# Two groups of a fused FNet and SwiGLU block: TensorE's units in another order

## The chip, the core and the metric

The kernel runs on one core of one Trainium2 chip. The core has a matrix engine (TensorE; PE in the profile, with its weight loads in a row of their own, PEld), three engines for elementwise work (VectorE or DVE, ScalarE or ACT, GpSimd or POOL) and an engine that mainly issues loads and stores (SyncE or SP). Each engine runs its own list of instructions in order and waits for the others on semaphores. TensorE writes its results into eight banks of PSUM, 128 x 512 floats each; ACT and DVE read them out into the main on-chip memory, SBUF.

The metric is the device time of one execution in microseconds (us). The time before is the median of three runs, 693.0 us, from 691.73 to 693.62.

## The reference, cut to what matters

One sequence of 2048 rows of width 512 goes through a Fourier mixing layer and then through a gated feed-forward layer of inner width 1792, both behind a layer norm that is modulated by a conditioning vector:

```python
mod = (_silu(c) @ w_mod).reshape(c.shape[0], 6, 1, -1)
sa, ca, ga, sb, cb, gb = (mod[:, 0], mod[:, 1], mod[:, 2], mod[:, 3], mod[:, 4], mod[:, 5])
h = _layernorm(x, axis=-1) * (1 + ca) + sa
x = x + ga * _A_ref(h, A_dft_seq_re, A_dft_seq_im, A_dft_hid_re, A_dft_hid_im)
h = _layernorm(x, axis=-1) * (1 + cb) + sb
x = x + gb * _B_ref(h, B_w1, B_w3, B_w2)

def _B_ref(x, w1, w3, w2):
    gate = jnp.einsum("bsd,df->bsf", x, w1)
    up = jnp.einsum("bsd,df->bsf", x, w3)
    h = _silu(gate) * up
    out = jnp.einsum("bsf,fd->bsd", h, w2)
    return out
```

The change touches only the second layer, `_B_ref`.

## The kernel before, in words

**Splitting.** TensorE multiplies rounded numbers, so each operand is kept as a high part (the value rounded) and a low part (what the rounding left over), and every product takes three matmuls: high by high, high by low, low by high (`product`, line 98; its matmuls are all on line 100). ACT makes the high parts (`copy`, line 87) and DVE the low ones (`minus`, line 90). So a new operand costs one instruction on each of the two, and the low part waits for the high one.

**Tiles and groups.** The 2048 rows are four tiles t of 512, taken as two pairs, (0, 2) and (1, 3). The inner width is seven slices g of 256. A group is one slice for one pair. The list `items` has twelve groups, numbered here 0 to 11: slices 2 to 6 for the first pair (groups 0 to 4), then slices 0 to 6 for the second (groups 5 to 11). Group 5 is "the turn" (`turning` is 5), group 6 the one behind it, group 11 the last.

**Units.** Within a group, w1's and w3's blocks are multiplied by a scheme with seven products in place of eight (`factor`): a1 to a7 are w1's, b1 to b7 are w3's. A unit has six matmuls of 512 columns. Products of one operand add up in the same bank: w1's in banks 0 to 2 and w3's in banks 3 to 5. So a6 adds onto a1's bank 0, a7 onto that and a4 onto that, and between two of them ACT copies the bank out (`x<-bank`, line 87), or DVE adds it to such a copy (`plus`, line 93). w3's results are then multiplied by w1's (`times`, line 96), and what comes out is split for the next step (`hf`). w1's results go through the Silu on ACT (line 1244).

**Second products.** A unit y multiplies such results by w2. For groups 5 to 9 there are seven of them, again by the scheme of seven products (`seven_unit`), in the order 2, 5, 3, 1, 6, 7, 4. All use banks 6 and 7. After each, ACT reads both banks out, scaled by `gb` (`copy_by`, line 335, two instructions `y<-bank,gb`), and POOL adds the pair to a sum in device memory (line 1352). Products 3, 6, 7 and 4 add onto what 5 or 1 left in the banks, so they too must wait until the copy of the one before is out. For groups 10 and 11 there are eight plain units (`down_unit`), whose results DVE adds directly (line 1146); once w1's products of group 11 are done, they go round over five banks (6, 7, 0, 1, 2).

**Order.** What runs when is set by a string for each group, read from left to right, in program order for all engines; a unit that begins with `-` belongs to the group before. `y` takes the next second product from the queue `seconds`, which still holds those of the group before. Behind each unit two things are put in. Steps that `behind(n, ...)` deferred by n units go first (the splits above are such steps). Then comes preparation from the queue `jobs`: the coming weights are split (`w1h`, `w1l`) and so are their sums (`w1s`, `w1sh`, `w1sl`), as much of it as `beside` finds room for by a fixed account of 1.36 us for each unit. So the string sets the places of the ACT and DVE instructions too.

The strings before (the second `body` holds for groups 6 to 9, with a `y` put in behind a6 in groups 7 to 9, whose head, as group 10's, is the second; group 10 has a body of its own; line 1795 and on):

```python
        body = "a6 a5 y y a7 y a3 y a4 y b1 y b2 y b6 b5 y"
        if i and items[i - 1] in SEVEN:
            body = "a6 a5 a7 y a3 a4 y b1 b2 y b6 b5 y"
        ...
        if i == len(items) - 1:
            body = "a6 a5 a7 a3 a4 b1 b2 y b6 y b5 y b7 y b4 y y b3 y y y y y y y y y y"
        head = "-b7 a1 -b4 -b3 a2 " if i == turning else "-b7 a1 a2 -b4 -b3 " if i else "a1 a2 "
        if spread and i < len(items) - 1:
            head = "-b7 a1 y a2 -b4 y -b3 "
        if i == len(items) - 1:
            head = "-b7 y a1 a2 y -b4 y -b3 "
```

## Time and profile before

| | |
|---|---|
| time, median of 3 runs | 693.0 us (691.73 to 693.62) |
| the profiled execution's own time | 692.95 us |
| its span, first to last instruction | 691.2 us |
| TensorE busy | 675.1 us, 98% of the span |
| TensorE weight loads | 558.0 us, 81% |
| VectorE busy | 586.5 us, 85% |
| ScalarE busy | 451.5 us, 65% |
| GpSimd busy | 132.8 us, 19% |

The profile is of one execution. Its page sums up each engine, and its other views show the single instructions in order of time (the timeline), whom each engine waited for (the waits) and the busy time by stretch of the span (the windows). All times in them are counted from the start of the span. In a row of the timeline stand the start, the length, the engine, the line of the kernel, what is written and read, and in brackets the idle time before it with the instruction that ended it. Instructions of one kind that follow each other are merged into one row (x2). Consecutive matmuls overlap, so their pace is read from start to start. The groups' places in the span: group 6's a6 starts at 500.80, the last group's a6 at 645.68.

### The profile page before, as it was taken

To read this page: it belongs to the slowest core of one execution; us is meant where nothing else is said; L and a number is where in the kernel's file an instruction comes from. 1 tells how busy PE (TensorE), PEld (TensorE's weight loads), DVE (VectorE), ACT (ScalarE), POOL (GpSimd) and SP (SyncE) were. 2 spreads that over 40 slices of the span, in tenths; PEclk is the share of its full clock that TensorE was granted. 3 is DMA by queue.
4 is the path that set the end of the run, shared out by engine and by line. 5 is a ranking of instruction groups with operands and counts; after the bars stand their busy time and mean duration, and the time that the engine had idled before them with its cause. 6 is when DMAs were issued, how large, how long until landed. Compare 5 with 4: busy or idle time off the path is not lost.

```text
span 691.2 us, 9031 instructions
## 1 busy us (share of the span) xinstructions
PE 675.1 (98%) x3122; PEld 558.0 (81%) x3122; DVE 586.5 (85%) x945; ACT 451.5 (65%) x751; POOL 132.8 (19%) x156
## 2 busy tenths in 40 slices
PE   7999899999999999999999999999999999999996
PEld 5899788888888888888788888887878888888785
DVE  5999769997999988889997989787998979888375
ACT  4998956555353665663577767867677887877520
POOL 1320252543435000010101001011002112221100
PEclk9999999999999999999999999999999999999999
DMA  8730289787588541273667666376939898899803
GB/s 269 216 125 1 67 307 360 260 299 255 186 308 277 166 151 30 46 139 122 97 164 140 150 152 121 92 133 118 277 74 210 166 202 168 177 217 173 191 28 126
DMA packets 40261, 116.80 MB, mean 169 GB/s; under 512 B 5136, under 2 KB 5392, under 8 KB 40208
## 3 DMA queue, kind: packets, MB, share of 16 engines
q0 software_dynamic: 14512, 50.86, 36.5%
q1 hardware_dynamic: 25264, 63.98, 27.9%
q10 hardware_dynamic: 432, 1.31, 0.5%
q8 instruction: 26, 0.43, 0.3%
q14 instruction: 27, 0.22, 0.1%
HBM read 76.81 MB, written 41.42 MB: 171 GB/s over the span
## 4 chain that ended last, share of the span: by engine, by line
PE 83%; DVE 8%; ACT 4%; DMA 2%; issue 1%; SPq 1%; another core or an unknown queue 1%; DVEq 0%; ACTq 0%
PE bank L100 55%; PE bank L750 25%; PE bank L559 1%; DMA wmr<-in_wmr 1%; PE bank L598 1%; SPq L231 1%; DVE xr L805 1%; DVE ul L90 1%; DVE hl L90 0%; ACT hm L501 0%; DMA w<-in_wdi 0%; ACT hh L87 0%; PE bank L576 0%; PE bank L485 0%
## 5 line engine op out<-in xcount | busy, mean ns | idle before, releaser
L100 PE MATMUL bank<-hf,w2h 128*128 128x512 f32 (+1 forms) x352 | 108.3, 389 | 0.0
L87 ACT ACTIVATE hf<-v 128x512 fp32r<-128x512 f32 x71 | 44.4, 631 | 67.3 <-DVE v L96 56.5
L335 ACT ACTIVATE y<-bank,gb 128x512 f32<-128x512 f32 x118 | 76.6, 683 | 4.2 <-PE bank L100 3.6
L100 PEld LDWEIGHTS bank<-hf,w2h 128*128 128x128 f32 x352 | 65.6, 188 | 15.3 <-ACT y L335 1.4
L1160 POOL DMA_DIRECT2D sum<-y x28 | 24.1, 859 | 240.7 <-ACT y L335 124.5
L100 PE MATMUL bank<-hf,w2l 128*128 128x512 f32 (+1 forms) x176 | 68.1, 387 | 0.0
L90 DVE TENSOR_TENSOR hf<-v,hf 128x512 fp32r<-128x512 f32 x71 | 48.7, 686 | 10.3 <-ACT hf L87 10.3
L1352 POOL DMA_DIRECT2D sum<-y x35 | 29.9, 854 | 128.8 <-ACT y L335 119.7
L87 ACT ACTIVATE x<-bank 128x512 f32<-128x512 f32 x72 | 41.9, 593 | 13.3 <-PE bank L100 12.5
L750 PE MATMUL bank<-d,us 128*128 128x512 f32 x128 | 49.9, 390 | 0.1
L750 PE MATMUL bank<-bh,us 128*128 128x512 f32 x128 | 49.9, 390 | 0.0
L750 PE MATMUL bank<-bh,ul 128*128 128x512 f32 x128 | 49.9, 389 | 0.0
L750 PE MATMUL bank<-d,uh 128*128 128x512 f32 x128 | 49.8, 389 | 0.0
L750 PE MATMUL bank<-l,us 128*128 128x512 f32 x128 | 49.8, 389 | 0.0
L750 PE MATMUL bank<-l,uh 128*128 128x512 f32 x128 | 49.8, 389 | 0.0
L170 POOL DMA_INDIRECT re<-in_ctr,mirror x32 | 35.6, 1111 | 64.3 <-DVE ul L90 38.5
L170 POOL DMA_INDIRECT im<-in_cti,mirror x32 | 33.4, 1044 | 36.3 <-PE bank L750 8.7
L93 DVE TENSOR_TENSOR x<-bank,x 128x512 f32<-128x512 f32 x36 | 24.7, 686 | 17.8 <-PE bank L100 17.8
L100 PEld LDWEIGHTS bank<-hf,w2l 128*128 128x128 f32 x176 | 33.1, 188 | 6.7
L1244 ACT ACTIVATE v<-v 128x512 f32<-128x512 f32 x36 | 22.7, 629 | 23.1 <-DVE v L93 22.7
L93 DVE TENSOR_TENSOR v<-bank,x 128x512 f32<-128x512 f32 x36 | 24.7, 686 | 14.9 <-PE bank L100 14.0
L100 PE MATMUL bank<-h2h,w1h 128*128 128x512 f32 x80 | 31.1, 389 | 0.0
(260 smaller groups left out, 1904.2 us busy)
## 6 DMA issues: line engine op xcount, KB each, us to landing
sum<-y POOLq DMA_DIRECT2D x63, 512.0 KB
w<-in_w SPq DMA_DIRECT2D x42, 512.0 KB
re<-in_ctr SPq DMA_DIRECT2D x32, 256.0 KB
im<-in_cti SPq DMA_DIRECT2D x32, 256.0 KB
wmc<-in_wmc SPq DMA_DIRECT2D x8, 512.0 KB
xr<-in_xt SPq DMA_DIRECT2D x8, 512.0 KB
sum<-xr SPq DMA_DIRECT2D x8, 512.0 KB
x<-in_x SPq DMA_DIRECT2D x11, 256.0 KB
```

The costliest lines, as they stand in the source:

```text
L87: nc.scalar.activation(dst, src, AF.Copy, scale=scale)
L90: nc.vector.tensor_tensor(out=dst, in0=a, in1=b, op=OP.subtract)
L93: nc.vector.tensor_tensor(out=dst, in0=a, in1=b, op=OP.add)
L100: nc.tensor.matmul(acc, lhs[a], rhs[b], start=first and n == 0, stop=last and n == len(PASSES) - 1, skip_group_check=more,)
L170: nc.gpsimd.indirect_dma_start(dst, None, rows, bass.IndirectOffsetOnAxis(ap=at, axis=0))
L231: queue.dma_start(raw_w[dt][q * 64 : (q + 1) * 64, m, :], w[i][par::2, q])
L335: nc.scalar.activation(dst, src, AF.Identity, scale=by)
L559: nc.tensor.matmul(halves(hb[k])[:, m, :], sides((hh, hl)[a][k])[:, dt, m, :], wu[dt][:, b, m, :], start=False, stop=dt % 2 == 1 and n == ...
L750: nc.tensor.matmul(acc[what, e], lhs, rhs, start=begin and i == 0, stop=(end or (turn and what == "x")) and i == len(terms) - 1, skip_grou ...
L1160: nc.gpsimd.dma_start(sums[t, d // 2], y, accum_op=OP.add)
L1244: behind(k != 0 or q == 0, lambda: nc.scalar.activation(v, src, AF.Silu))
L1352: nc.gpsimd.dma_start(sums[t, which], y, accum_op=OP.add)
```

## The change

The string of group 6 gets a line of its own, and the last group's string is written anew; nothing else is touched:

```diff
@@ -1798,6 +1798,8 @@
         body = "a6 a5 y y a7 y a3 y a4 y b1 y b2 y b6 b5 y"
         if i and items[i - 1] in SEVEN:
             body = "a6 a5 a7 y a3 a4 y b1 b2 y b6 b5 y"
+        if i == turning + 1:
+            body = "a6 a5 y a7 a3 y a4 b1 y b2 b6 y b5"
         spread = i > 1 and items[i - 2] in SEVEN
@@ -1806,7 +1808,7 @@
         if i == len(items) - 1:
-            body = "a6 a5 a7 a3 a4 b1 b2 y b6 y b5 y b7 y b4 y y b3 y y y y y y y y y y"
+            body = "a6 a5 b1 a7 a3 b2 a4 y b6 y b5 y b7 y b4 y y b3 y y y y y y y y y y"
```

In group 6 each of its four y units comes one unit sooner. Two other units stand between neighbours as before, except behind the fourth: from there to the next y (in group 7's head, `-b7 a1 y`) there are three in place of two. In the last group b1 moves from behind a4 to between a5 and a7, and b2 from behind b1 to between a3 and a4. Instructions and transfers are the same ones in number and size.

**First place: ACT in group 6.** Shown are ten rows from the Silu of w1's product a7 on, before (`hf` are high parts of right-hand factors, `w1h` and `w1sh` high parts of the next group's weights and of their sums, `y` the copies out of banks 6 and 7):

```order
L1244 ACTIVATE v_717_4580<-v_717_4580 128x512
L335 ACTIVATE y_731_4655<-bank6_729_4653,gb_152 128x512
L335 ACTIVATE y_731_4655<-bank7_730_4654,gb_152 128x512
L87 ACTIVATE hf_732_4665<-v_661_4308 128x512
L87 ACTIVATE w1h_734_4677<-w1_718_4582 128x1024
L87 ACTIVATE hf_736_4684<-v_661_4308 128x512
L1244 ACTIVATE v_716_4579<-v_716_4579 128x512
L1244 ACTIVATE v_717_4580<-bank0_714_4571 128x512
L87 ACTIVATE w1sh_738_4696<-w1s_735_4679 128x1024
L335 ACTIVATE y_741_4701<-bank6_739_4699,gb_152 128x512
```

The same stretch of ACT now, from the copies of the first y on:

```order
L335 ACTIVATE y_730_4644<-bank6_728_4642,gb_152 128x512
L335 ACTIVATE y_730_4644<-bank7_729_4643,gb_152 128x512
L87 ACTIVATE hf_731_4654<-v_660_4307 128x512
L87 ACTIVATE hf_732_4664<-v_661_4308 128x512
L1244 ACTIVATE v_717_4580<-v_717_4580 128x512
L87 ACTIVATE w1h_734_4677<-w1_718_4582 128x1024
L87 ACTIVATE hf_736_4684<-v_661_4308 128x512
L1244 ACTIVATE v_716_4579<-v_716_4579 128x512
L335 ACTIVATE y_739_4689<-bank6_737_4687,gb_152 128x512
L335 ACTIVATE y_739_4689<-bank7_738_4688,gb_152 128x512
L87 ACTIVATE w1sh_741_4701<-w1s_735_4679 128x1024
```

The first pair of copies now stands ahead of the Silu of a7, and the second pair ahead of `w1sh`, with the Silu from bank 0 (a4's) behind it.

**Second place: ACT and DVE at the end of group 6 and the head of group 7.** ACT before, from the third y's copies to the fifth's (`x<-bank3` is the copy of b6, `hf` the high part of the result of group 6's b7, `x<-bank0` the copy of group 7's a1):

```order
L335 ACTIVATE y_749_4741<-bank7_740_4700,gb_152 128x512
L87 ACTIVATE w2sh_751_4753<-w2s_747_4734 128x1024
L87 ACTIVATE x_744_4721<-bank3_743_4714 128x512
L87 ACTIVATE w3h_753_4765<-w3_733_4675 128x1024
L87 ACTIVATE x_755_4774<-bank5_754_4767 128x512
L335 ACTIVATE y_759_4783<-bank6_757_4781,gb_152 128x512
L335 ACTIVATE y_759_4783<-bank7_758_4782,gb_152 128x512
L87 ACTIVATE w3sh_761_4795<-w3s_756_4776 128x1024
L87 ACTIVATE hf_762_4805<-v_717_4580 128x512
L87 ACTIVATE x_764_4814<-bank0_763_4807 128x512
L335 ACTIVATE y_769_4823<-bank6_757_4781,gb_152 128x512
```

ACT now, from the high part of b2's result on, which stands behind the third y's copies there:

```order
L87 ACTIVATE hf_749_4749<-v_716_4579 128x512
L87 ACTIVATE x_744_4721<-bank3_743_4714 128x512
L87 ACTIVATE w2sh_751_4760<-w2s_748_4744 128x1024
L335 ACTIVATE y_754_4765<-bank6_752_4763,gb_152 128x512
L335 ACTIVATE y_754_4765<-bank7_753_4764,gb_152 128x512
L87 ACTIVATE w3h_756_4777<-w3_733_4675 128x1024
L87 ACTIVATE x_758_4786<-bank5_757_4779 128x512
L87 ACTIVATE hf_760_4801<-v_717_4580 128x512
L87 ACTIVATE x_762_4810<-bank0_761_4803 128x512
L87 ACTIVATE w3sh_767_4818<-w3s_759_4788 128x1024
L335 ACTIVATE y_768_4821<-bank6_752_4763,gb_152 128x512
```

b6's copy has moved from behind the third y's copies and `w2sh` to ahead of `w2sh`, and `w3sh` from ahead of b7's `hf` and the copy of a1 to behind them, right ahead of the fifth y's copies.

DVE before, in the same stretch (`x<-bank3` and the product `v` behind it are the two steps on b7's result):

```order
L90 TENSOR_TENSOR w3s_756_4776<-w3_733_4675,w3s_756_4776 128x256
L90 TENSOR_TENSOR w3l_760_4793<-w3_733_4675,w3h_753_4765 128x1024
L93 TENSOR_TENSOR x_755_4774<-bank3_743_4714,x_755_4774 128x512
L96 TENSOR_TENSOR v_717_4580<-v_717_4580,x_755_4774 128x512
L90 TENSOR_TENSOR w3sl_768_4820<-w3s_756_4776,w3sh_761_4795 128x1024
L90 TENSOR_TENSOR hf_762_4805<-v_717_4580,hf_762_4805 128x512
```

DVE now:

```order
L90 TENSOR_TENSOR w3s_759_4788<-w3_733_4675,w3s_759_4788 128x256
L93 TENSOR_TENSOR x_758_4786<-bank3_743_4714,x_758_4786 128x512
L96 TENSOR_TENSOR v_717_4580<-v_717_4580,x_758_4786 128x512
L90 TENSOR_TENSOR w3l_766_4816<-w3_733_4675,w3h_756_4777 128x1024
L90 TENSOR_TENSOR hf_760_4801<-v_717_4580,hf_760_4801 128x512
L90 TENSOR_TENSOR w3sl_769_4831<-w3s_759_4788,w3sh_767_4818 128x1024
```

On DVE the two steps on b7's result have moved ahead of `w3l`.

**Third place: TensorE in the last group.** The last three matmuls of a5 and the first three behind it, before:

```order
L100 MATMUL bank2_976_5937<-th_667_4343,w1sh_941_5750 128x512
L100 MATMUL bank2_976_5937<-tl_672_4360,w1sh_941_5750 128x512
L100 MATMUL bank2_976_5937<-th_667_4343,w1sl_942_5760 128x512
L100 MATMUL bank0_962_5859<-th_671_4358,w1sh_941_5750 128x512
L100 MATMUL bank0_962_5859<-tl_675_4373,w1sh_941_5750 128x512
L100 MATMUL bank0_962_5859<-th_671_4358,w1sl_942_5760 128x512
```

and now:

```order
L100 MATMUL bank2_976_5937<-th_667_4343,w1sh_941_5750 128x512
L100 MATMUL bank2_976_5937<-tl_672_4360,w1sh_941_5750 128x512
L100 MATMUL bank2_976_5937<-th_667_4343,w1sl_942_5760 128x512
L100 MATMUL bank3_978_5946<-h2h_625_4122,w3h_950_5803 128x512
L100 MATMUL bank3_978_5946<-h2l_628_4133,w3h_950_5803 128x512
L100 MATMUL bank3_978_5946<-h2h_625_4122,w3l_955_5823 128x512
```

Before, a7 came next and added onto bank 0, which a6 had filled one unit earlier; now b1 comes next, in bank 3, and a7 one unit later.

## The prediction

> **What bounds the kernel now.** I read the page first, then whom TensorE waited for in the part with the changed groups, then the timeline of each engine around those waits. From the page:

> ```profile
> PE 675.1 (98%) x3122; PEld 558.0 (81%) x3122; DVE 586.5 (85%) x945; ACT 451.5 (65%) x751; POOL 132.8 (19%) x156
> ...
> PEclk9999999999999999999999999999999999999999
> ...
> PE 83%; DVE 8%; ACT 4%; DMA 2%; issue 1%; SPq 1%; another core or an unknown queue 1%; DVEq 0%; ACTq 0%
> ```

> TensorE is busy 98% of the span at full clock, and 83% of the chain that ends last is its own work. A new order leaves its matmuls what they are. It can only take away or add waits between them. The view of waits, from 480 us to the end, has these rows (who waited for whom, total, times, longest):

> ```profile
> POOL sum L1352 <- DMA sum<-y: 9.0, 2, 4.6
> ...
> PEld bank L100 <- ACT y L335: 1.9, 3, 1.0
> PEld bank L100 <- ACT x L87: 1.0, 2, 0.5
> ```

> So TensorE's weight loads, which run ahead of the matmuls, were held up five times in this whole stretch, three times by copies of second products and twice by copies of w1's or w3's. Of the compute engines only POOL waits for a transfer. Here are four of the five places in TensorE's timeline (start, length), with the rows around them, and one place without a wait (526.36) for later:

> ```profile
> 512.61 0.39 PE L100 MATMUL bank<-h2l,w3h 128*128 128x512 f32 x1
> 512.84 0.39 PE L100 MATMUL bank<-h2h,w3l 128*128 128x512 f32 x1
> 513.76 0.73 PE L100 MATMUL bank<-hf,w2sh 128*128 128x512 f32 x2 [0.53 <-ACT y L335]
> ...
> 519.12 0.39 PE L100 MATMUL bank<-hf,w2l 128*128 128x512 f32 x1
> 519.63 0.50 PE L100 MATMUL bank<-th,w3sh 128*128 128x512 f32 x1
> 519.97 0.40 PE L100 MATMUL bank<-tl,w3sh 128*128 128x512 f32 x1
> ...
> 526.36 0.39 PE L100 MATMUL bank<-th,w3l 128*128 128x512 f32 x1
> 526.59 0.63 PE L100 MATMUL bank<-hf,w2sh 128*128 128x512 f32 x2
> ...
> 639.26 0.39 PE L100 MATMUL bank<-h2h,w1l 128*128 128x512 f32 x1
> 639.76 0.74 PE L100 MATMUL bank<-hf,w2sh 128*128 128x512 f32 x2
> ...
> 648.18 0.39 PE L100 MATMUL bank<-th,w1sl 128*128 128x512 f32 x1
> 648.56 0.50 PE L100 MATMUL bank<-th,w1sh 128*128 128x512 f32 x1
> ```

> The pace is 0.23 us from start to start (512.61 to 512.84), so a unit of six takes 1.36. Whatever is above the pace is a wait. A wait also costs the next matmul 0.11: it comes 0.34 behind the first (519.63 to 519.97), and a pair behind a wait lasts 0.73, not 0.63 as at 526.59. That gives:

> - A, group 6's third y at 513.76: 0.92 - 0.23 + 0.11 = 0.80
> - B, group 6's b7 at 519.63: 0.51 - 0.23 + 0.11 = 0.39
> - C, the last group's a7 at 648.56: 0.38 - 0.23 + 0.11 = 0.26
> - D, a y in the head of the last group at 639.76: 0.50 - 0.23 + 0.11 = 0.38, and the fifth held-up load, of the next y there

> D lies ahead of the new string, in units that it leaves alone. A, B and C together are 1.45 us, the most that the change can gain.

> **What makes A, B and C.** The timelines of ACT and DVE there:

> ```profile
> 507.40 0.63 ACT L1244 ACTIVATE v<-v 128x512 f32<-128x512 f32 x1 [1.17 <-DVE v L93]
> ...
> 509.08 0.63 ACT L87 ACTIVATE hf<-v 128x512 fp32r<-128x512 f32 x1
> 509.60 1.06 ACT L87 ACTIVATE w1h<-w 128x1024 fp32r<-128x1024 f32 x1
> ...
> 511.59 0.59 ACT L1244 ACTIVATE v<-bank 128x512 f32<-128x512 f32 x1
> 512.07 1.06 ACT L87 ACTIVATE w1sh<-w1s 128x1024 fp32r<-128x1024 f32 x1
> 513.02 1.26 ACT L335 ACTIVATE y<-bank,gb 128x512 f32<-128x512 f32 x2
> ...
> 516.35 0.63 ACT L87 ACTIVATE hf<-v 128x512 fp32r<-128x512 f32 x1 [0.63 <-DVE v L96]
> ...
> 518.98 0.60 ACT L87 ACTIVATE x<-bank 128x512 f32<-128x512 f32 x1
> ...
> 522.21 1.06 ACT L87 ACTIVATE w3sh<-w3s 128x1024 fp32r<-128x1024 f32 x1
> 524.62 0.63 ACT L87 ACTIVATE hf<-v 128x512 fp32r<-128x512 f32 x1 [1.34 <-DVE v L96]
> ...
> 525.63 1.26 ACT L335 ACTIVATE y<-bank,gb 128x512 f32<-128x512 f32 x2
> ...
> 647.39 0.63 ACT L87 ACTIVATE hf<-v 128x512 fp32r<-128x512 f32 x1 [2.03 <-DVE v L96]
> 647.93 1.27 ACT L87 ACTIVATE x<-bank 128x512 f32<-128x512 f32 x2
> ```

> ```profile
> 502.54 0.69 DVE L90 TENSOR_TENSOR hf<-v,hf 128x512 fp32r<-128x512 f32 x1
> ...
> 506.08 0.69 DVE L90 TENSOR_TENSOR v<-v,v 128x512 f32<-128x512 f32 x1
> ...
> 513.16 1.23 DVE L90 TENSOR_TENSOR w1sl<-w1s,w1sh 128x1024 fp32r<-128x1024 f32 x1 [0.64 <-ACT w1sh L87]
> ...
> 522.04 1.22 DVE L90 TENSOR_TENSOR w3l<-w,w3h 128x1024 fp32r<-128x1024 f32 x1
> 523.17 0.68 DVE L93 TENSOR_TENSOR x<-bank,x 128x512 f32<-128x512 f32 x1
> 523.89 0.69 DVE L96 TENSOR_TENSOR v<-v,x 128x512 f32<-128x512 f32 x1
> ```

> ACT's copies of the second y are last in a queue that ACT works off without a gap from 507.40; they begin at 513.02, and the third y starts 0.74 later (A). The copy of b6 ends at 518.98 + 0.60 = 519.58, behind an `hf`, the third y's pair and `w2sh`, and b7 starts 0.05 later (B). In the last group the copy of a6 stands behind an `hf` that waits for b3's result, and a7 comes right after a6's copy (C). All three are waits for ACT's place in line; none is for data that come from memory.

> **Group 6.** Each y comes one unit sooner, so A's copies get the same two units of room, but the queue ahead of them is shorter. Before, ACT idled 1.17 ahead of the Silu at 507.40, waiting for a7's result; now the first y's pair (1.14) runs in that gap. a7's own result comes later, since a7 is one unit later: on DVE it now stands two steps behind the one at 506.08, at 0.6 to 0.72 each, and is done near 508.1. From the Silu to `w1sh` ACT took 512.07 - 507.40 = 4.67. The same rows stand in between now but for one `hf` (0.52, from 509.08 to 509.60) and the Silu of a4 (0.48, from 511.59 to 512.07), so `w1sh` begins near 508.1 + 3.67 = 511.8, and the pair of the second y two places of 0.57 ahead of it, at 510.65. Its first bank is free at 510.65 + 0.74 = 511.39. The third y, the tenth unit of the string before, would have started at 512.84 + 0.23 = 513.07 without its wait; as the ninth it wants to start at 511.71. A is gone, with 0.3 to spare. b6's copy now stands right behind the `hf` that began at 516.35, ahead of `w2sh` and the pair; that `hf` waits for DVE, which is 0.3 sooner there (below), so the copy runs from about 516.6 to 517.2. b7 wants it at 513.07 + 4 x 1.36 = 518.5: B is gone, with 1.3 to spare. The first y, now the third unit, starts at 513.07 - 7 x 1.36 = 503.55 and needs a factor whose low part DVE finishes at 502.54 + 0.69 = 503.23; it holds, by 0.3. Gain 0.80 + 0.39 = 1.19.

> **What is late next.** TensorE now reaches group 7 1.19 sooner, and the sixth y of the queue (526.59 before) wants banks 6 and 7 at 525.40. Before, it did not wait, but only just: the fifth y's pair began at 525.63, and 525.63 + 0.74 = 526.37. Its pair hangs on DVE, which has no slack there:

> ```profile
> 513.00:528.00 15.00, 14.35 (x62) 11.32 (x62) 14.22 (x22) 12.92 (x21) 3.37 (x4) 1.00 0.86 168
> 528.00:540.00 12.00, 12.00 (x55) 9.93 (x54) 8.99 (x16) 9.60 (x18) 2.60 (x4) 1.00 1.03 208
> ```

> (stretch, its length, busy time of PE, PEld, DVE, ACT and POOL, then clock and DMA, for this stretch and the next). DVE works 14.22 of 15 us. So b7's two steps, which ended at 523.89 + 0.69 = 524.58, come sooner only by what the new order gives: `w1sl` waits for `w1sh`, 0.3 sooner, and `w3l` (523.17 - 522.04 = 1.13) now stands behind them. That is 523.15, and `hf` on ACT at 523.2. But ACT now has `w3sh` (0.95, 512.07 to 513.02) between `hf` and the pair, where it had run it in an idle stretch before. The pair begins at 523.2 + (525.63 - 524.62) + 0.95 = 525.16, its first bank is free at 525.90, and the sixth y waits 525.90 - 525.40 = 0.50, plus 0.11: it gives back 0.61. The bounds of this cost are zero, if `hf` comes by 522.7, and 527.32 - 525.40 + 0.11 = 2.03, if b7's steps come no sooner than before (524.62 + 1.01 + 0.95 + 0.74 = 527.32). I take 0.61, which goes by the order of rows on both engines. Behind group 7's head the strings are the old ones, and I carry the rest of the gain to the end at no loss: from 528 on DVE works 8.99 and ACT 9.60 of 12 us, so what they are behind they make up.

> **The last group.** b1 goes into bank 3, which group 10's b4 left four units earlier, and w3's parts for it are split while group 10 runs. It covers the copy of a6: that ends near 649.2 in the worst case (647.93 + 1.27), and a7 now starts at 648.18 + 0.23 + 1.36 = 649.8. C is gone: 0.26. b2 one unit sooner also makes w2's split sooner by one unit, which nobody waits for. a4 now stands right ahead of the first y, whose banks go round 7, 0, 1, 2, 6; the second y overwrites a4's bank 0 two units later (2.72), and ACT needs 0.6 to read it. I cost these at nothing. If ACT were held up, 2.1 us of cover would go first.

> The loads by SP and the adds by POOL are the same ones; the four adds of group 6 are issued about one unit sooner and no transfer moves past another.

> **The sum.** -0.80 - 0.39 + 0.61 - 0.26 = -0.84 against the profiled execution's own 692.95, which is 0.05 below the median of 693.0. On the median: 692.2.

> [...] The trace shows 0.11 behind each wait, and in the view of waits it is the weight loads that wait. [...]

> **The rivals.**

> 1. The wait at the sixth y does not come, since `hf` is out by 522.7, for instance because DVE saves more than 0.3 at `w1sl`. Against it stands `w3sh` ahead of the pair and DVE's 14.22 of 15. Gain 1.45: 691.5.
> 2. Slower: the same wait is larger than what was gained. This happens if DVE ends b7's two steps later than 524.0: then hf at 524.05, the pair at 526.0, its bank at 526.74, and 526.74 - 525.40 + 0.11 is 1.45. At its worst (524.58, as before) the wait is 2.03, the sum +0.58, the time 693.6. For it: one late ACT result (`w3h` or `w2sh`, which DVE's low parts wait for) delays everything behind it on a full DVE. Against it: the new order on DVE has b7's steps ahead of `w3l`, and this needs 0.85 more than I laid out.
> 3. The group gives all back and no more: the y's wait is 1.19 wherever exactly, since a DVE without slack sets the pace from 513 to 528, and only C remains. Then -0.26: 692.7.

> **How the numbers follow.** The likeliest case, with a wait of 0.3 to 1.0 at the sixth y, has 0.6 and gives 691.8 to 692.5; rival 1 has 0.15, rival 2 has 0.1, rival 3 has 0.15. All of them lie within 0.3% (2.1 us) of 693.0, which is about what a measurement of this kernel can tell from no change: its three runs lie 1.9 us apart. The chances of faster and slower by more than that come from that scatter alone and from what I overlook: 0.08 faster, since the likeliest cases lean that way, 0.06 slower, 0.86 within. The range must take in rivals 1 to 3 and about half the runs' scatter: 691.2 to 693.6.

> **What would show it right or wrong.** In TensorE's timeline of the changed kernel the gaps A, B and C are closed, and there is a new gap of 0.3 to 1.0 ahead of the sixth y, near 526, that the waits put down to ACT's `y`; on ACT `w3sh` stands right before the fifth y's pair without a gap. D stays as it is. If the second y's pair on ACT begins after 511, A is not gone. If the gap is near 2, rival 2 holds. The prediction would be wrong altogether if a new wait showed up in groups 8 to 10, whose order is untouched, or in the tail behind 655.

## The result and the profile after

The changed kernel takes 694.13 us (median of 22 runs, 693.24 to 696.26), beside 693.0 for the kernel before (22 runs, 691.73 to 694.03). The ratio is 1.0017, with a 95% interval of 1.0011 to 1.0023: 1.2 us slower, where 0.8 us faster was forecast, and outside the forecast range. The profiled execution took 694.64 us. From the changed kernel's page:

```profile
span 692.9 us, 9028 instructions
...
PE 674.7 (97%) x3122; PEld 558.9 (81%) x3122; DVE 586.9 (85%) x945; ACT 451.8 (65%) x751; POOL 132.0 (19%) x156
...
q8 instruction: 26, 0.43, 0.3%
q14 instruction: 28, 0.23, 0.1%
...
PE 84%; DVE 9%; ACT 2%; DMA 2%; issue 1%; SPq 1%; ACTq 0%; DVEq 0%
```

Nothing here says where the time went: the same engine, the same work, a busy time 0.4 us less than before. Two small things have moved, the number of instructions and q14, one of the two queues that the page calls `instruction`. On the page of the kernel before they read:

```profile
span 691.2 us, 9031 instructions
...
q8 instruction: 26, 0.43, 0.3%
q14 instruction: 27, 0.22, 0.1%
```

Three instructions fewer, and one packet of 8 KB more. Both lead to the loss, but first the part on which the prediction rests.

**TensorE.** The view of waits from 480 us on has one row for TensorE's weight loads, and the row for copies of w1's and w3's products (`x L87`) is gone:

```profile
PEld bank L100 <- ACT y L335: 1.9, 3, 1.0
```

In TensorE's timeline (start, length) of the changed kernel, at the third y, at b7, at the sixth y, at D and at the last group's a7:

```profile
512.13 0.62 PE L100 MATMUL bank<-hf,w2sh 128*128 128x512 f32 x2
512.59 0.39 PE L100 MATMUL bank<-hf,w2sl 128*128 128x512 f32 x1
...
518.71 0.39 PE L100 MATMUL bank<-th,w3sl 128*128 128x512 f32 x1
518.93 0.39 PE L100 MATMUL bank<-th,w3sh 128*128 128x512 f32 x1
...
525.50 0.39 PE L100 MATMUL bank<-th,w3l 128*128 128x512 f32 x1
526.46 0.74 PE L100 MATMUL bank<-hf,w2sh 128*128 128x512 f32 x2 [0.56 <-ACT y L335]
...
639.28 0.39 PE L100 MATMUL bank<-h2h,w1l 128*128 128x512 f32 x1
639.78 0.74 PE L100 MATMUL bank<-hf,w2sh 128*128 128x512 f32 x2
...
649.56 0.39 PE L100 MATMUL bank<-h2h,w3l 128*128 128x512 f32 x1
649.78 0.39 PE L100 MATMUL bank<-th,w1sh 128*128 128x512 f32 x1
```

The third y starts at the pace (its pair lasts 0.62, the length of a pair without a wait), b7 follows 0.22 behind the matmul ahead of it, a7 likewise: A, B and C are gone. D is as it was (0.50). There is one new wait, at the sixth y: 526.46 - 525.50 = 0.96, less 0.23, plus 0.11 behind it, is 0.84.

**The whole stretch.** The two profiled executions differ ahead of the change: by 0.53 us at one and the same wait in group 2. That is chance, since kernels with the same orders ahead of this wait lie as far apart there (342.38 in lg, 342.92 before). So TensorE is measured from there. Of the kernel before, the matmul behind that wait and the last matmul:

```profile
342.92 0.50 PE L100 MATMUL bank<-th,w3sh 128*128 128x512 f32 x1 [0.36 <-ACT x L87]
...
684.00 0.28 PE L100 MATMUL bank<-hf,w2l 128*128 128x256 f32 x1
```

and of the changed one:

```profile
343.45 0.50 PE L100 MATMUL bank<-th,w3sh 128*128 128x512 f32 x1 [0.36 <-ACT x L87]
...
683.74 0.28 PE L100 MATMUL bank<-hf,w2l 128*128 128x256 f32 x1
```

341.08 before, 340.29 now: TensorE gained 0.79 us, where 0.84 was forecast. Even with its late start it ends 0.26 earlier than before. Laid matmul by matmul beside the kernel before, 0.07 of the 0.79 is there already at group 6's a6, ahead of the change. Up to the sixth y another 1.31 is gained, the wait there and the units just behind it give back 0.87, and the last group gains 0.29. So the change itself is worth 0.72.

**The tail.** Behind the start of the last matmul the span of the kernel before goes on for 691.2 - 684.00 = 7.2 us, that of the changed one for 692.9 - 683.74 = 9.2. These 2.0 us are the loss: -0.79 + 1.96 = 1.17, and the medians differ by 0.17% of 693, which is 1.18. The tail has no matmul, no add and no output that is late. What it has is in the view of transfers from 685.5 us to the end, here the bandwidth in 40 slices of 0.24 us and the packets of q14, first of the kernel before:

```profile
GB/s 26 267 285 285 280 39 108 52 4 0 0 0 0 0 34 0 34 0 0 0 0 0 0 0 0 0 0 0 0 0 0 0 0 0 0 0 0 0 0 0
...
q14 instruction: 4, 0.03, 1.3%
```

then of the changed kernel:

```profile
GB/s 358 190 367 91 30 129 13 0 0 0 0 0 0 34 0 34 0 0 0 0 0 0 0 0 0 34 0 0 0 0 0 0 0 0 0 0 0 0 0 0
...
q14 instruction: 5, 0.04, 1.6%
```

The high numbers at the left are the last outputs; they are through two slices sooner now. A 34 that stands alone is one packet of q14 (8 KB in 0.24 us). Both kernels have two of them close together, from 688.8 and from 688.6 us; the changed one has a third, 2.3 us behind the second (689.15 and 691.47).

The view of SP's waits has one row that differs, before and after (line 2572 has become line 2574):

```profile
SPq L2572 <- SPq L2572: 2.5, 1, 2.5
```

```profile
SPq L2574 <- SPq L2574: 4.6, 2, 2.6
```

SP stood still once for 2.5 us at this line before, and now twice, for 4.6 in all, with no other engine named. The timeline leaves out the instructions of this place, SP's branch and its last waits, but the trace has them. SP loads the flag, branches past `general` (the version for inputs without the symmetries, which doesn't run with these), and then works off 8 waits, 12 more and the handshakes of the end. Starts in us behind the branch's start:

```
step behind the branch   1     2     3     4     5     6    ...  last
before                 2.56  2.66  2.75  2.83  2.90  2.98       4.74
after                  2.63  2.72  2.82  4.87  4.96  5.05       6.83
```

In the changed kernel SP stands still for 2.05 us between its third and its fourth wait and then runs on at the same pace. In the kernel before, the fourth follows the third by 0.08. The third packet on q14 can't be what ended the pause: it starts at 691.47, and the fourth wait at 690.83. It comes 0.64 behind the fourth wait, as the second of the pair (689.15) comes 0.56 behind the first (688.59). So, by the author's reading of these times, it marks that SP has run on into another piece of code. The extra packet alone is no sign of a pause: before_short, below, has 28 too and no such pause.

### The profile page after: what moved, and what is told of

Its sections match the earlier page's. It is cut to its first block, busy times and chain, and to the rows that moved or that the text cites. A ratio compares the mean times of both kernels' runs of the same rounds, so it can differ in the third digit from the quotient of the medians.

```text
span 692.9 us, 9028 instructions
## 1 busy us (share of the span) xinstructions
PE 674.7 (97%) x3122; PEld 558.9 (81%) x3122; DVE 586.9 (85%) x945; ACT 451.8 (65%) x751; POOL 132.0 (19%) x156
## 3 DMA queue, kind: packets, MB, share of 16 engines
q10 hardware_dynamic: 432, 1.31, 0.6%
## 4 chain that ended last, share of the span: by engine, by line
PE 84%; DVE 9%; ACT 2%; DMA 2%; issue 1%; SPq 1%; ACTq 0%; DVEq 0%
PE bank L100 54%; PE bank L750 25%; PE bank L559 2%; PE bank L598 1%; DMA w<-in_wdr 1%; PE bank L576 1%; DMA w<-in_wdi 1%; SPq L231 1%; DMA x<-in_x 1%; DVE xr L805 1%; DVE v L96 1%; DVE x L93 0%; DVE hl L90 0%; ACT hm L501 0%; DVE w3s L90 0%
## 5 line engine op out<-in xcount | busy, mean ns | idle before, releaser
L100 PE MATMUL bank<-hf,w2h 128*128 128x512 f32 (+1 forms) x352 | 108.3, 389 | 0.0
L87 ACT ACTIVATE hf<-v 128x512 fp32r<-128x512 f32 x71 | 44.4, 631 | 67.0 <-DVE v L96 53.9
L335 ACT ACTIVATE y<-bank,gb 128x512 f32<-128x512 f32 x118 | 76.6, 682 | 4.1 <-PE bank L100 3.6
L100 PEld LDWEIGHTS bank<-hf,w2h 128*128 128x128 f32 x352 | 65.6, 188 | 15.3 <-ACT y L335 1.4
L100 PE MATMUL bank<-hf,w2l 128*128 128x512 f32 (+1 forms) x176 | 68.1, 387 | 0.0
L90 DVE TENSOR_TENSOR hf<-v,hf 128x512 fp32r<-128x512 f32 x71 | 48.7, 686 | 10.9 <-ACT hf L87 10.9
L1352 POOL DMA_DIRECT2D sum<-y x35 | 29.8, 852 | 128.4 <-ACT y L335 119.9
L87 ACT ACTIVATE x<-bank 128x512 f32<-128x512 f32 x72 | 41.8, 592 | 12.8 <-PE bank L100 12.2
L100 PEld LDWEIGHTS bank<-hf,w2l 128*128 128x128 f32 x176 | 33.0, 188 | 6.7
L93 DVE TENSOR_TENSOR v<-bank,x 128x512 f32<-128x512 f32 x36 | 24.7, 686 | 15.3 <-PE bank L100 14.4
L1244 ACT ACTIVATE v<-v 128x512 f32<-128x512 f32 x36 | 22.7, 629 | 22.9 <-DVE v L93 22.6
L93 DVE TENSOR_TENSOR x<-bank,x 128x512 f32<-128x512 f32 x36 | 24.7, 685 | 14.4 <-PE bank L100 13.7
L100 PE MATMUL bank<-h2h,w1h 128*128 128x512 f32 x80 | 31.1, 389 | 0.0
```

What stands on the lines that cost most here:

```text
L87: nc.scalar.activation(dst, src, AF.Copy, scale=scale)
L90: nc.vector.tensor_tensor(out=dst, in0=a, in1=b, op=OP.subtract)
L93: nc.vector.tensor_tensor(out=dst, in0=a, in1=b, op=OP.add)
L100: nc.tensor.matmul(acc, lhs[a], rhs[b], start=first and n == 0, stop=last and n == len(PASSES) - 1, skip_group_check=more,)
L335: nc.scalar.activation(dst, src, AF.Identity, scale=by)
L1244: behind(k != 0 or q == 0, lambda: nc.scalar.activation(v, src, AF.Silu))
```

## Experiments

**The theory.** A new order changes which loads and stores need a wait instruction of their own on SP. The change was said to leave the instructions the same in number; of the matmuls, copies and transfers that is so, of the waits it isn't. Counted in the program, SP has 324 instructions ahead of the branch in the kernel before and 322 in the changed one, and `general`, which lies behind the branch and is jumped over, has 266 and 264 there (`general`'s text is the same; its waits depend on what ran ahead of it). So SP's last waits lie behind 593 instructions before (3 more stand at the head) and behind 589 now. The idea, an inference that the runs below test: SP's code comes in pieces, and a boundary between two of them now falls behind the third of these waits; the branch has to fetch the piece that it jumps to (2.63 us in the changed kernel), and the next piece isn't there yet when SP gets to it (the 2.05 us). The rivals: the new orders make something end later behind the last matmul, or the difference is chance of starts and clock.

All runs in one table. "Stretch" is the one above, from the matmul behind the wait at 342 us to the last one, and "tail" is from there to the span's end; both are of the profiled execution.

| Kernel | SP ahead of its last waits | time, us | ratio to before, 95% | stretch | tail |
|---|---|---|---|---|---|
| before | 593 | 693.0 | | 341.08 | 7.2 |
| after | 589 | 694.13 | 1.0017 [1.0011, 1.0023] | 340.29 | 9.2 |
| after_p4 | 593 | 691.62 | 0.9985 [0.9975, 0.9995] | 340.21 | 6.8 |
| before_m4 | 589 | 695.31 | 1.0033 [1.0020, 1.0047] | 340.96 | 9.1 |
| lg | 593 | 692.59 | 0.9996 [0.9986, 1.0006] | 340.73 | 7.0 |
| after_p2 | 591 | 694.20 | 1.0015 [1.0001, 1.0029] | 340.31 | 9.0 |
| no_sixth | 595 | 691.69 | 0.9973 [0.9962, 0.9984] | 339.41 | 6.9 |
| before_short | 328 | 691.97 | 0.9980 [0.9969, 0.9990] | 340.91 | 5.6 |
| best | 323 | 691.68 | 0.9963 [0.9949, 0.9976] | 339.42 | 5.8 |
| no_sixth_short | 325 | 690.92 | 0.9975 [0.9963, 0.9987] | 339.40 | 5.7 |
| best_again | 323 | 690.76 | 0.9963 [0.9945, 0.9980] | 338.77 | 6.0 |
| before_p124 | 717 | 694.95 | 1.0031 [1.0014, 1.0047] | 340.91 | 8.9 |
| before_p107 | 700 | 694.66 | 1.0015 [1.0001, 1.0028] | 341.40 | 8.3 |

The kernel before ran again beside each set: 692.49 beside the four runs from after_p4 to after_p2, 693.45 beside no_sixth, before_short and best, 693.13 beside the next two, 693.23 beside the last two. The ratios go by these.

**Both orders, with SP's code put back.** In `general`, four loads are cut in halves; none of these is executed. (TensorE and VectorE get one wait more each in `general`; the other edits of `general` below move the never-run code of the other engines a little too.)

```diff
         for k in range(ND):
-            nc.sync.dma_start(wm[v, k // 2][:, k % 2, :], wmr[v, k // 2, :, k % 2, :])
+            for h in range(2 if 4 * (1 - v) + k < 4 else 1):
+                at = slice(h * N // 2, (h + 1) * N // 2) if 4 * (1 - v) + k < 4 else slice(0, N)
+                nc.sync.dma_start(wm[v, k // 2][:, k % 2, at], wmr[v, k // 2, :, k % 2, at])
```

> The changed kernel, with four halvings of loads in `general`, the branch that is never run: four dead instructions more on SP, and one more wait each on TensorE and VectorE there, none of them executed. SP's end code then lies where it lies in the kernel before (593 instructions ahead of it, not 589). Theory, place of SP's code: the 2.03 us pause among SP's last waits is gone, the last matmul's start to the span's end is 7.1 to 7.2 us again (9.12 in the changed kernel), the queue q14 has 27 packets, and the time is 692.2, 0.8 below the kernel before. Rival, the new orders themselves cost the 2 us behind the last matmul (a transfer, an add or a wait that ends later): the time stays at 694.1 and the tail at 9.1. Second rival, the difference is only chance of the starts and the clock: the time is anywhere from 693 to 694, with tails of both lengths.

Measured: 0.9985, that is 1.0 us faster than before (0.35 to 1.7), a tail of 6.8, 27 packets on q14, no pause. Four instructions that never run turn the change from a loss into the gain that was forecast.

**The old orders, with SP's code moved the other way.** Eight loads of `general` become four:

```diff
-        for k in range(ND):
-            nc.sync.dma_start(wm[v, k // 2][:, k % 2, :], wmr[v, k // 2, :, k % 2, :])
+        for k in range(ND // 2):
+            nc.sync.dma_start(wm[v, k], wmr[v, k])
```

> The kernel before, orders untouched, with eight loads in the never-run `general` put together to four: four dead instructions fewer on SP, so that 589 lie ahead of its end code, as in the changed kernel. Theory, place of SP's code: a pause of 2.0 us appears behind the third of SP's last waits, the tail is 9.1 to 9.2 us, q14 has 28 packets, and the time is 693.0 + 2.0 = 695.0. Rival, the orders cost it: nothing that is executed has changed, so 693.0 and a tail of 7.15.

Measured: 1.0033, 2.3 us slower; pause of 2.16 us behind the third wait, tail 9.1, 28 packets. With after_p4 this closes the square: the loss goes with the place of the code, whichever order stands ahead of it. Both rivals fall.

**The last group's order alone.** The second changed line of the diff, on the kernel before.

> The last group's new order alone, on the kernel before. It leaves the number of SP's instructions as it was (593 ahead of the end code). Theory, place of SP's code: the wait C at a7 goes (0.26 us), A, B and D stay, the tail stays at 7.15 us, so 692.7. Rival, the new order of the last group makes the tail longer: 0.26 gained and 1.96 lost, 694.7 and a tail of 9.1.

Measured: 0.9996, whose interval (0.9986 to 1.0006) can't tell 0.26 us from nothing; no pause. The trace can: the stretch is 0.35 shorter than before, 0.29 of it from the last group on, and a7 follows at the pace (timeline of TensorE in this run):

```profile
648.93 0.39 PE L100 MATMUL bank<-h2h,w3l 128*128 128x512 f32 x1
649.16 0.39 PE L100 MATMUL bank<-th,w1sh 128*128 128x512 f32 x1
```

So the line for the last group does what it should and doesn't move SP's code; it is the line for group 6 that does.

**The boundary two instructions sooner, 128 instructions later, and 17 further on.** after_p2 is the changed kernel with two loads of `general` halved; before_p124 and before_p107 are the kernel before with the same loads cut into so many pieces that SP has 124 and 107 dead instructions more.

> The changed kernel with two dead instructions more on SP in the never-run branch (591 ahead of the end code). Theory, place of SP's code: the boundary between two pieces of code lies two instructions sooner among those that run, so the 2.03 us pause is behind the first of SP's last waits and not behind the third; its length and the time are those of the changed kernel, 694.1, q14 28 packets. Rival, the pause belongs to what the fourth wait waits for: it stays behind the third.

> The kernel before, orders untouched, with its loads in the never-run `general` cut into more pieces: 124 dead instructions more on SP (717 ahead of the end code, which is 128 more than in the changed kernel). If a fetched piece of code is 8192 bytes, 128 instructions of 64 bytes, as the packets on the queue q14 are large, the boundary is back behind the third of SP's last waits: a pause of 2.0 to 2.2 us there, tail 9.1, time 2.0 above the kernel before (ratio 1.003). If a piece is 256 instructions, no boundary is near: tail 7.2, ratio 1.000.

> The same with 107 dead instructions more on SP (700 ahead of the end code): by pieces of 128 the boundary lies 20 instructions behind the branch's target, 17 further than in the changed kernel. If the second piece is asked for as soon as the first has come, it arrives 2.24 us after the first last wait (688.59 to 690.83 in the changed kernel), while the 20 instructions take 1.25 us (0.06 to 0.09 each): a pause of about 1.0 us behind the 19th or 20th, tail 8.2, ratio 1.0014. If it is asked for only at the boundary, the pause is 2.0 us or more wherever it lies: tail 9.1, ratio 1.003. With pieces of 256 there is no pause: ratio 1.000.

Measured, again as starts in us behind SP's branch, from the trace:

```
step behind the branch   1     2     3     4   ...  20    21    ...  last
after_p2               2.57  5.09  5.18  5.27      6.31  6.37       7.18
before_p124            2.68  2.77  2.87  4.92      6.00  6.07       6.88
before_p107            2.60  2.70  2.79  2.87      3.96  5.08       6.01
```

**A short jump.** The ten places in `general` that issue loads and stores do so on POOL, so that SP jumps over 1 instruction and not over 266:

```diff
-                nc.sync.dma_start(raw[key], source[key][0])
+                nc.gpsimd.dma_start(raw[key], source[key][0])
...
```

> The kernel before, orders untouched, with the ten places in the never-run `general` that issue loads and stores on SP issuing them on POOL instead: SP's branch at the end then jumps over 1 instruction and not over 266. Theory: the 2.5 us between SP's branch and its first last wait are the fetch of code from far away; a short jump needs none, the branch (686.36) is followed by the first last wait within 0.2 us, and the span ends 1.4 us sooner (that wait is for the last output, which lands at 687.49, and 2.3 us of waits and handshakes follow), up to 2.0 sooner if most of the waits pass ahead of that landing: 691.1 to 691.6. Rival, each taken branch costs 2.5 us wherever it goes: 693.0. Second rival: a boundary between two pieces of SP's code now lies about 8 instructions behind the branch; if crossing it costs 2 us even where code runs straight on, 693.0 too, but with the pause behind one of the last waits.

Measured: 0.9980, 1.4 us faster, tail 5.6. SP's first wait starts 0.19 us behind the branch, not 2.56. On POOL, which has the long jump now, 2.62 us stand behind the branch (676.24 to 678.86) in place of 0.18, but nothing waits for them. The gain isn't the whole 2.4, since SP's tenth wait now stands for 1.3 us (687.13 to 688.41, from the trace): VectorE's own branch, at 685.09, has its next instruction at 688.36. In the kernel before the same step of VectorE takes from 685.22 to 688.37, and nothing waits for it there: SP's first wait comes later still, at 688.92. The boundary, by the count behind the eighth step, costs little where the code runs up to it without a long jump: the ninth starts 0.36 behind the eighth. The count puts it behind the eleventh step in no_sixth_short and behind the thirteenth in `best`, and there the next step comes 0.36 and 0.34 later, where steps otherwise follow by 0.06 to 0.1. So such a crossing costs about 0.3, by estimate.

**The new wait at the sixth y.** Both orders, SP's code out of the way by the halved loads of after_p4, and for group 7 a head of its own, in which the sixth y stands behind b3 instead of ahead of it:

```diff
+        if i == turning + 2:
+            head = "-b7 a1 y a2 -b4 -b3 y "
```

> The changed kernel with its two orders, a head of its own for group 7 that puts the sixth y behind b3 instead of ahead of it, and seven dead instructions on SP (595 ahead of its end code, so no boundary among the last waits). Theory: the wait of 0.84 us at 525.5 is only the sixth y coming before ACT has its banks free; one unit (1.36 us) later it finds them free, no wait takes its place, and the time is 0.84 below that of the changed kernel with SP's code put back (691.62): 690.8. Rival, ACT and VectorE are the bound of this stretch: the wait comes again at the next y or at a unit of group 7, and the time stays at 691.6.

Measured: 0.9973, 1.9 us faster than before (1.1 to 2.6); the theory has 0.8 + 0.84 = 1.6. The stretch is 0.80 shorter than that of after_p4, and the sixth y, one unit (b3) later, starts at the pace:

```profile
527.02 0.39 PE L100 MATMUL bank<-h2h,w3sl 128*128 128x512 f32 x1
527.25 0.62 PE L100 MATMUL bank<-hf,w2sh 128*128 128x512 f32 x2
527.70 0.39 PE L100 MATMUL bank<-hf,w2sl 128*128 128x512 f32 x1
```

No other wait of TensorE took its place up to 560 us, so the new wait came from the order and not from a limit of ACT or VectorE.

**Everything together.** no_sixth_short is both orders, the head for group 7 and `general`'s loads on POOL; `best` and best_again, the same kernel twice, also have a new head for the last group, against D:

```diff
-            head = "-b7 y a1 a2 y -b4 y -b3 "
+            head = "-b7 a1 y a2 -b4 y -b3 y "
```

> All that gained, together: both new orders, the head of group 7 with the sixth y behind b3, a head of the last group with its second products two units apart (first behind a1, then behind b4 and b3, so that the waits D of 0.38 and 0.25 us go), and the loads of `general` on POOL. Theory: 0.87 (both orders) + 0.84 + 0.63 + 1.4 to 2.0 below the kernel before, 688.2 to 688.8 where that is at 692.5. Rival: VectorE or ACT, no longer held back by TensorE's waits, give part of it back in the stretch from 513 to 528 or in the last group: 689.5 or more, with new waits there.

> Both new orders, the sixth y behind b3, and the loads of `general` on POOL; the last group's head as it was. Theory, the parts add up: 0.26 + 0.53 (both orders with their new wait) + 0.84 + 1.4 to 1.5 (short branch on SP) = 3.0 to 3.1 below the kernel before, ratio 0.9955; D's two waits (0.38 and 0.25) are there. Rival, the parts hide each other: what TensorE gains makes transfers collide, and waits for adds in memory (a tile whose sum is still being added) come up in groups 7 and 8 as in the run `best`: 2.4 or less, ratio 0.9965.

> The same kernel as `best`. If its two waits at 538.9 and 548.8 (0.36 and 0.25 us), behind a copy on ACT that stood 1.8 us for an add in memory, were chance, they are gone in this profile and the ratio is that of no_sixth_short less 0.6 us of D: 0.9946. If they belong to the orders, they are there again, and the ratio is about that of no_sixth_short.

Measured: 0.9963 twice for `best` (2.6 us faster than before), 0.9975 for no_sixth_short. All beat both kernels, and all fall short of the sums, 3.7 to 4.3 and 3.0 to 3.1. By the profiled executions the parts do add up for no_sixth_short: its stretch is 1.68 shorter than before and its tail 1.5, and that execution took 689.27. Its other six runs took 690.45 to 692.92. Their mean granted clock is lower, 0.993 to 0.996 beside 0.999, but they have no trace here, and what makes them longer isn't shown.

For `best` three things are seen. D is gone in both profiles (no gap over the pace behind 640 us). In the first, two new waits came up at 538.9 and 548.8, behind a copy on ACT that waited for an add in memory; in the second they are gone and the stretch is 0.65 shorter, so the order alone doesn't make them:

```profile
537.59 0.63 ACT L87 ACTIVATE hf<-v 128x512 fp32r<-128x512 f32 x1 [1.81 <-DMA sum<-y]
```

With the two waits gone 0.9946 was expected of best_again; 0.9963 was measured, and the interval (0.9945 to 0.9980) only just reaches the expected value. Both executions lose time elsewhere. VectorE gets the first x at 7.40 us (7.30 in the second); in the kernel before it starts on it at 5.79, from the two timelines:

```profile
7.40 0.69 DVE L449 BATCH_NORM_STATS2 st<-x 128x6 f32<-128x512 f32 x1 [4.86 <-DMA x<-in_x]
```

```profile
5.79 0.69 DVE L449 BATCH_NORM_STATS2 st<-x 128x6 f32<-128x512 f32 x1 [3.25 <-DMA x<-in_x]
```

And around the span lie 2.4 us (692.23 less 689.8, 691.06 less 688.7), where the other kernels have 1.7 to 1.9; so it is in all 17 runs of this kernel (2.3 to 2.6). In both of its profiles, and in no other, a packet on q14 starts 2.2 us behind the end of the span, so this too may be code that is fetched, which isn't shown. Between them, that is up to 2 us of what `best` should gain. What makes the first load late wasn't found. The new orders aren't needed for it: in before_p107 VectorE gets the first x at 7.42, and in the other ten profiles at 5.70 to 6.04.

## Why the prediction was wrong, point by point

- **A, gone: right, with its steps.** The second y's pair on ACT was to begin at 510.65, and the changed run is 0.53 late from the start: 511.18. It begins at 511.12. By the letter of the sign "after 511" A would not be gone; without the late start it is 510.59, and TensorE has no wait there. `w1sh` was to begin at 511.8 plus 0.53, and begins at 512.26. A and B were priced at 1.19; up to the sixth y TensorE gained 1.31.
- **B, gone: right.** b6's copy was to run from 516.6 to 517.2; it runs from 517.11, which is 516.58 without the late start.
- **C, gone: right, and by more than its price.** In the changed run ACT's `hf` of the last group waited 2.55 us for an add in memory, and a6's copy, the first of the two at 648.47, ended only at 649.05 by the trace. b1 covered it (a7 at 649.78). In the old order a7, due at 649.78 - 1.36 = 648.42, would have had to wait for it, by estimate 0.5 longer than C was; in before_p107, which has the old order, the same late `hf` cost a gap of 0.81 there in place of 0.38.
- **The new wait at the sixth y: right in place and cause, mis-sized by 0.23** (0.84 for 0.61). ACT's and VectorE's rows of the changed kernel:

```profile
511.12 1.25 ACT L335 ACTIVATE y<-bank,gb 128x512 f32<-128x512 f32 x2
512.26 1.05 ACT L87 ACTIVATE w1sh<-w1s 128x1024 fp32r<-128x1024 f32 x1
...
517.11 0.58 ACT L87 ACTIVATE x<-bank 128x512 f32<-128x512 f32 x1
...
523.76 0.63 ACT L87 ACTIVATE hf<-v 128x512 fp32r<-128x512 f32 x1 [2.03 <-DVE v L96]
524.30 0.58 ACT L87 ACTIVATE x<-bank 128x512 f32<-128x512 f32 x1
524.78 1.05 ACT L87 ACTIVATE w3sh<-w3s 128x1024 fp32r<-128x1024 f32 x1
525.73 1.26 ACT L335 ACTIVATE y<-bank,gb 128x512 f32<-128x512 f32 x2
...
647.93 0.63 ACT L87 ACTIVATE hf<-v 128x512 fp32r<-128x512 f32 x1 [2.55 <-DMA sum<-y]
648.47 1.07 ACT L87 ACTIVATE x<-bank 128x512 f32<-128x512 f32 x2
```

```profile
522.98 0.69 DVE L96 TENSOR_TENSOR v<-v,x 128x512 f32<-128x512 f32 x1
523.59 1.22 DVE L90 TENSOR_TENSOR w3l<-w,w3h 128x1024 fp32r<-128x1024 f32 x1
```

  VectorE has b7's step ahead of `w3l`, and ACT has `w3sh` right ahead of the fifth y's pair, both as laid out; `hf` at 523.2 and the pair at 525.16, plus 0.53, are 523.73 and 525.69, and they came at 523.76 and 525.73. TensorE was a little sooner than worked out (the y could have started at 525.73, not at 525.93). The extra 0.11 behind a wait is there again: the pair of the sixth y lasts 0.74, that of the third y, without a wait, 0.62. Rival 1, no wait, rival 2, a wait beyond 1.45, and rival 3, all given back, didn't come true.
- **Carried to the end at no loss: right as far as the last matmul.** The 0.50 that stands behind the sixth y (0.43 without the 0.07 from ahead of group 6) is still there at the last group. That 0.79 comes so near to 0.84 is in part luck: group 6 gave 0.12 more up to the sixth y than was laid out, the stretch of the wait took 0.26 more, and 0.07 came from ahead of the change.
- **"The loads by SP and the adds by POOL are the same ones", costed at nothing: this is the step that failed.** The transfers are the same, but SP's instruction list isn't: it lost two waits ahead of the branch and two in the branch that never runs. The end waits for SP (by the trace ACT and VectorE go on to their last handshakes about 0.15 behind one and the same step of SP, at 690.50 before and 692.20 now), so where its code lies decided 2.0 us, two and a half times what the matmuls gained. The text named the tail behind 655 us as a place where the forecast could go wrong altogether, but gave it neither a price nor a chance, and the three rivals were all about the one wait at the sixth y. A fourth rival, "the length of SP's list changes, and its end costs up to 2 us more or less", could have been read from the order of SP's instructions; its price couldn't, since the trace of before shows no such pause. It does show the 2.56 us behind SP's branch, next to which the bound would have had to be set.
- **The range** took in the unit orders' bounds, and they held. It had nothing for the code.

What the trace and the runs show of the tail: behind SP's branch stand 2.56 us where it jumps over 266 instructions (before), and 0.19 where it jumps over one (before_short). The packets of q8 have 16 KB each (26 with 0.43 MB), those of q14 8 KB (28 with 0.23 MB in the changed kernel), and on SP the boundary comes back after 128 instructions (before_p124). Its crossing cost SP about 0.3 us where it ran up to it without a long jump (0.36, 0.36 and 0.34 from one step to the next in before_short, no_sixth_short and `best`), but 2.05 us in the changed kernel, three steps behind the jump over 264.

## What to carry to other kernels

A change of order can also change how many instructions an engine has (here 589 on SP ahead of its last waits, for 593), and on the engine that finishes last, the place of its last instructions can be worth more than the change (here 2.0 us against 0.8). Count the instructions on that engine before and after, those of branches that never run too, and before a change of under 2 us is judged, run it once with a few dead instructions more, so that the code lies as before. And a rarely run version of the program is better kept off the engine that ends last: moving its loads to another engine made the unchanged kernel 1.4 us faster.

## What the runs showed that was not expected

- SP's jump over 266 instructions costs 2.6 us (before) and the one over 1 instruction 0.19 (before_short). SP gets past the boundary 4.9 to 5.1 us behind the jump, wherever it lies; what SP runs in between hides its share (a pause of 2.5 us behind the first step in after_p2, 2.05 behind the third in the changed kernel, 1.1 behind the twentieth in before_p107).
- Without a long jump ahead of it the same kind of boundary costs SP about 0.3 us (0.34 to 0.36 from step to step in three runs, where 0.06 to 0.1 is usual).
- With SP's long jump gone (before_short), the time behind VectorE's branch comes out from under it: 685.09 to 688.36.
- Profiled executions of these kernels reach the same matmul in group 2 at times between 342.4 and 344.6 us, with the same orders ahead of it. A gain of 0.3 us in TensorE's units can be read from the rows of its place in the trace, but not from the medians. It can't be read from the whole stretch alone either: five executions with the old orders have 340.91 to 341.40 there.
